# A gated linear attention with an MLP behind it: q and k of the later blocks transposed by DMA instead of by TensorE

## The chip, the cores and the metric

The kernel runs on one core of a Trainium2 chip. A core has four engines that compute (TensorE, or PE, for matmuls; VectorE, or DVE; ScalarE, or ACT; GpSimd, or POOL), a fifth, SyncE (SP), that only issues transfers and waits, and 16 DMA engines that all queues share. Every engine runs its own instructions in order. The metric is the device time of one execution in microseconds (us), lower is better.

## What is computed

For 4 batches and 8 heads of size 48, over 768 steps, a state of 48 by 48 is decayed row by row and updated, and read with q. The outputs of the 8 heads, side by side (384 numbers per token, 3,072 tokens), go through an MLP with a squared ReLU:

```python
for t in range(S):
    state = alpha[:, :, t, :, None] * state + np.einsum('bhd,bhe->bhde', k[:, :, t], v[:, :, t])
    y[:, :, t] = np.einsum('bhd,bhde->bhe', q[:, :, t], state)
...
h = x @ w_in                     # 384 -> 2048
r = np.maximum(h, 0.0)
g = s * (r * r) + b
return (g @ w_out).astype(np.float32)   # 2048 -> 384
```

Inputs and output are float32; the kernel computes its matmuls in bfloat16.

## The kernel before

The 768 steps of a batch are cut into 6 chunks of 128 steps, which makes 24 blocks n of 128 tokens (n // 6 is the batch, n % 6 the chunk). Within a block the recurrence is done in parallel form, and between the blocks of one batch a state is carried on. Names in capitals: NBLK is 24, NCH is 6, NP is 4 (pairs of heads), NLD is 8 (depth of the rings of loads).

For one block the steps are functions, each with one or a few engines:

- `load(n)`: four DMAs from SyncE, alpha, k, q and v, of 192 KB each, in pieces of 192 bytes (one head of one token).
- `ln` (ScalarE), `cum` (one matmul with a triangle of ones, and two exponentials on ScalarE into `bi_sb` and `b_sb`): the running product of the decays and its inverse. For blocks from the sixth on, `cum` ends with `decay(n)`: the last row of `b_sb` is stored to a row in DRAM and fetched back, spread over partitions, as `blast`; three small DMAs from SyncE, the second and third of which wait for the first to land. The last chunk of a batch needs none.
- `vcast` (GpSimd): v to bfloat16.
- `qk` (VectorE): k times `bi_sb` into `kb_sb` and q times `b_sb` into `qb_sb`, each 128 tokens by 8 heads of 64 columns (48 used).
- `tr`: eight transposes on TensorE (L244), four pairs of heads for q and four for k, into the PSUM tile `ct_ps`, and one copy on VectorE (L249) into `qkT_sb`.
- `amat`: eight matmuls from `qkT_sb` (L259) and two multiplications by a mask on VectorE (L267).
- `y` (`yp` and `st`): what the block reads from the carried state (L278) and from itself (L287), the block's contribution to the state (L298), the eviction of y on ScalarE (L305, `y_bf`), and the update of the state on VectorE (L334) and GpSimd (L339, L343), which reads `blast`.
- `xt`: three transposes of `y_bf` and an eviction on ScalarE into `xd_all`.
- `m(n, u)`, u from 0 to 3: the first product of the MLP (`mp`, L365, 12 matmuls), ReLU on ScalarE (`rl`, L379) and the square on VectorE (`sq`, L386).
- `o(n, u)`: the second product (`mm2`, L402, 4 matmuls). After u = 3 a block below the fourteenth is copied by ScalarE into `keep_sb`, which lies over the float32 staging of the first weights; it gets its bias later by `add_bias` (VectorE, L441) and is stored then. Later blocks get their bias from PSUM at once (VectorE, L415) and are stored. All stores were issued by SyncE (L438); the last block's two halves too (L435).

The order is written out by hand: the first blocks as a list, and from the fifth on by positions, `p = 8 * n` for the y of block n, and every other step at an offset from it. The steps are sorted by position and issued; each engine gets its part of that order, and a framework puts the semaphores between engines. For n of 8 and up the offsets are: `ln` p - 16.7, `cum` p - 14.8, `qk` p - 14.6, `tr` p - 10.8, `amat` p - 7.9, `load(n + 5)` p - 4, `y` p, `xt` p + 1, `m` p + 2.5, 3.5, 5.5 and 7.5, `o` p + 8.5, 9.5, 12.5 and 14.5. So one block's attention overlaps the MLP of the two blocks ahead of it. `add_bias` and the stores of the first 13 blocks stand at fixed positions from 117.3 and 118.2 on, 5.5 apart.

Of the kernel before, what the change touches and what calls it, by code (L numbers as in the profile page):

```python
# [9 lines left out]
BF16 = mybir.dt.bfloat16  # L10
# [4 lines left out]
def kernel(  # L15
# [25 lines left out]
    UNITS = 5  # L41
    assert sum(GROUPS) == NBLK
    NLD = 8

    ctx.enter_context(tc.manual_schedule())
    sb = ctx.enter_context(tc.tile_pool(name="sb", bufs=1))
# [32 lines left out]
    la_sb = ring("la_sb", [128, H, 64], BF16, 2)  # L79
    b_sb = ring("b_sb", [128, H, 48], FP32, 2)  # L80
    bi_sb = ring("bi_sb", [128, H, 48], FP32, 2)
    qb_sb = ring("qb_sb", [128, H, 64], BF16, 2)
    kb_sb = ring("kb_sb", [128, H, 64], BF16, 3)
    v_bf = ring("v_bf", [128, H, 48], BF16, 3)
    y_bf = ring("y_bf", [128, H * 48], BF16, 2)
    qkT_sb = ring("qkT", [128, 2, NP, 128], BF16, 2)
    am_sb = [ring("am_a", [128, NP, 128], BF16, 2), ring("am_b", [128, NP, 128], BF16, 2)]
    blast = ring("blast", [128, NP, 1], FP32, 3)
    row_dr = [dr.tile([1, H * 48], FP32, name=f"row_dr{i}") for i in range(3)]
# [118 lines left out]
    def cum(n):  # L208
        la = la_sb[n % 2]
        nc.tensor.matmul(out=cum_ps, lhsT=U_bf, rhs=la[:, :, 0:48], start=True, stop=True)  # L210
# [12 lines left out]
        if n < NCH - 1:  # L223
            nc.scalar.activation(out=blast[n % 3][0:112, :, 0], in_=tot_ps[0:112], func=AF.Exp)
        elif n % NCH < NCH - 1:
            decay(n)

    def decay(n):
        row = row_dr[n % 3]
        nc.sync.dma_start(out=row, in_=b_sb[n % 2].rearrange("s h d -> s (h d)")[127:128])  # L230
        for e in range(2):
            nc.sync.dma_start(
                out=blast[n % 3][64 * e : 64 * e + 48, :, 0],
                in_=row.rearrange("o (p e d) -> e d (o p)", e=2, d=48)[e],
            )

    def qk(n):
        nc.vector.tensor_tensor(out=kb_sb[n % 3][:, :, 0:48], in0=k_sb[n % NLD], in1=bi_sb[n % 2], op=ALU.mult)  # L238
        nc.vector.tensor_tensor(out=qb_sb[n % 2][:, :, 0:48], in0=q_sb[n % NLD], in1=b_sb[n % 2], op=ALU.mult)  # L239

    def tr(n):
        for x, t in ((0, qb_sb[n % 2]), (1, kb_sb[n % 3])):
            for p in range(NP):
                nc.tensor.transpose(  # L244
                    out=t_ps[0:112, x, p, :],
                    in_=t.rearrange("a h d -> a (h d)")[:, 128 * p : 128 * p + 112],
                    identity=ident,
                )
        nc.vector.tensor_copy(  # L249
            out=qkT_sb[n % 2][0:112].rearrange("a x p t -> a (x p t)"),  # L250
            in_=t_ps[0:112].rearrange("a x p t -> a (x p t)"),
        )

    def amat(n):
        qkT = qkT_sb[n % 2]
        for p in range(NP):
            for e in range(2):
                r0 = 64 * e
                nc.tensor.matmul(  # L259
                    out=a_ps[e][:, p, :],  # L260
                    lhsT=qkT[r0 : r0 + 48, 1, p, :],
                    rhs=qkT[r0 : r0 + 48, 0, p, :],
                    start=True,
                    stop=True,
                )
        for e in range(2):
            nc.vector.tensor_tensor(out=am_sb[e][n % 2], in0=a_ps[e], in1=mask4, op=ALU.mult)  # L267
# [6 lines left out]
    def yp(n):  # L274
        c = n % NCH
        if c > 0:
            for p in range(NP):
                nc.tensor.matmul(  # L278
                    out=y_ps[:, 96 * p : 96 * p + 96],
                    lhsT=qkT_sb[n % 2][0:112, 0, p, :],  # L280
                    rhs=sd_sb[(n - 1) % 2][0:112, p, :],
                    start=(p == 0),
                    stop=False,
                    skip_group_check=True,
                )
        for h in range(H):
            nc.tensor.matmul(  # L287
                out=y_ps[:, 48 * h : 48 * h + 48],
                lhsT=am_sb[h % 2][n % 2][:, h // 2, :],
                rhs=v_bf[n % 3][:, h, :],  # L290
                start=(c == 0 and h == 0),
                stop=(h == H - 1),
                skip_group_check=True,
            )
        if c < NCH - 1:
            kb = kb_sb[n % 3].rearrange("a h d -> a (h d)")
            for p in range(NP):
                nc.tensor.matmul(  # L298
                    out=pst[:, p, :],
                    lhsT=kb[:, 128 * p : 128 * p + 128],  # L300
                    rhs=v_bf[n % 3][:, 2 * p : 2 * p + 2, :],
                    start=True,
                    stop=True,
                )
        nc.scalar.activation(out=y_bf[n % 2], in_=y_ps[:, 0 : H * 48], func=AF.Copy)  # L305
# [88 lines left out]
    def mm2(g, t, u):  # L394
# [14 lines left out]
        if u == 3:  # L409
            if g < NKEEP:  # L410
                nc.scalar.activation(out=keep_sb[g], in_=op[:, 0:d_model], func=AF.Copy)
                return
            ot = out_sb[nout[0] % 3]
            nout[0] += 1
            nc.vector.tensor_tensor(out=ot, in0=op[:, 0:d_model], in1=bias_w, op=ALU.add)  # L415
            store(g, ot)


    def last(u):
# [14 lines left out]
                nc.vector.tensor_tensor(out=ot[:, 0:hc], in0=op[half][:, 0:hc], in1=bias_w[:, cols], op=ALU.add)  # L434
                nc.sync.dma_start(out=out[(NBLK - 1) * C : NBLK * C, cols], in_=ot[:, 0:hc])  # L435

    def store(n, o):
        nc.sync.dma_start(out=out[n * C : (n + 1) * C, :], in_=o)  # L438

    def add_bias(n):  # L440
        nc.vector.tensor_tensor(out=keep_sb[n], in0=keep_sb[n], in1=bias_w, op=ALU.add)  # L441
# [21 lines left out]
    for t in la_sb:  # L463
        nc.vector.memset(t, 0.0)
    nc.vector.memset(ones_c, 1.0)
    for t in qb_sb + kb_sb + blast:
        nc.vector.memset(t, 0.0)
    make_identity(nc, ident)
    for i in range(NP):
# [8 lines left out]
    def at(pos, fn, *args):  # L478
        events.append((pos, len(events), fn, args))
# [54 lines left out]
        at(111.5 + 2 * i, bias_row, i)  # L534
    for n in range(NKEEP):
        at(117.3 + 5.5 * n, add_bias, n)
        at(118.2 + 5.5 * n, store, n, keep_sb[n])
    for u in range(1, 4):
        at((30.5, 31.2, 32.5)[u - 1], o, 3, u)
    at(20.0, load, NLD)  # L540
    for n in range(4, NBLK):
        p = 8 * n
        if n > 4:
            f = min((n - 5) / 3.0, 1.0)
            c, t, a = 9.0 + 5.8 * f, 5.8 + 5.0 * f, 3.4 + 4.5 * f
# [12 lines left out]
        at(p + 1.0, xt, n)  # L558
    for _, _, fn, args in sorted(events, key=lambda e: e[:2]):
        fn(*args)  # L560
# [30 lines left out]
```

## Time and profile before

| what | value |
|---|---|
| time, median of 3 runs | 199.65 us (199.53 to 199.88) |
| profiled execution: span from first to last instruction | 198.2 us |
| what the median lies above that span | 1.45 us |
| TensorE busy | 185.2 us, 93% |
| VectorE busy | 150.8 us, 76% |
| ScalarE busy | 118.8 us, 60% |
| GpSimd busy | 64.2 us, 32% |
| bytes moved by DMA | 30.33 MB, 153 GB/s in the mean |
| transposes of q and k on TensorE (L244) | 192 matmuls, 19.9 us busy, pipelined |
| copies of them on VectorE (L249) | 24, 685 ns each |

The profiled execution's own time is known by its span only. A page of the profile gives the busy time by engine, the span in 40 slices, the DMA queues, the chain that ended last, and the costliest groups of instructions. In the lines, PE is TensorE's matmul, PEld its weight load, DVE, ACT, POOL and SP the other engines; a q behind the name (SPq, ACTq) is the engine's sequencer, which issues transfers and waits. "x8" is the number of instructions in a line; "L244" is a line of the kernel. A line of the chain or the timeline begins with its start in us from the span's start and its length in us.

### The profile page before, as it was taken

The numbers are of one execution on the slowest core, as the hardware profiler recorded it, in microseconds if no ns is written. First come the engines' busy times: TensorE is split into PE (matmuls) and PEld (weight loads), VectorE is DVE, ScalarE is ACT, GpSimd is POOL, SyncE is SP. The second block draws the span as 40 slices with busy tenths as digits, with TensorE's granted clock in tenths as the row PEclk, the third lists the DMA queues.
The fourth block names the chain that finished last, engine by engine and source line by source line (L and its number), as shares of the span: only waits on it lengthen the run. The fifth ranks groups of instructions, "written<-read, shape, count | busy, mean of one in ns | idle before, by whom it ended". The sixth has DMA issues, their size and how long they took to land.

```text
span 198.2 us, 6120 instructions
## 1 busy us (share of the span) xinstructions
PE 185.2 (93%) x2440; PEld 145.3 (73%) x2440; DVE 150.8 (76%) x296; ACT 118.8 (60%) x243; POOL 64.2 (32%) x96
## 2 busy tenths in 40 slices
PE   1999899988899999999999999999999999999994
PEld 1566587754577688888878877878888877877783
DVE  5467777867466779789877996989987999998532
ACT  3245668381675765766766677666575665664650
POOL 5142251611120136326500633623700851652000
PEclk9999999999999999999999999999999999999999
DMA  7999999999999384693968846958947953122212
GB/s 125 189 342 232 314 283 369 199 177 193 187 172 195 60 142 86 101 159 64 195 84 148 134 68 120 159 93 193 229 87 164 161 176 112 41 82 81 87 37 79
DMA packets 113454, 30.33 MB, mean 153 GB/s; under 512 B 106627, under 2 KB 111890, under 8 KB 113426
## 3 DMA queue, kind: packets, MB, share of 16 engines
q1 hardware_dynamic: 109262, 29.15, 73.7%
q10 hardware_dynamic: 4164, 0.79, 2.8%
q8 instruction: 19, 0.31, 0.7%
q14 instruction: 9, 0.07, 0.1%
HBM read 25.19 MB, written 4.74 MB: 151 GB/s over the span
## 4 chain that ended last, share of the span: by engine, by line
PE 68%; SPq 15%; DMA 10%; DVE 3%; ACT 1%; issue 1%; ACTq 0%; DVEq 0%
PE h_ps L365 25%; PE o_ps L402 25%; DMA q_sb<-in_q_dram 8%; SPq L128 5%; PE ct_ps L244 5%; SPq L147 4%; PE a_ps L259 3%; SPq L125 3%; SPq L122 2%; PE ct_ps L210 2%; PE y_ps L287 2%; PE h_ps L312 2%; DMA al_sb<-in_alpha_dram 2%; SPq L131 1%; PE a_ps L425 1%; PE y_ps L278 1%
## 5 line engine op out<-in xcount | busy, mean ns | idle before, releaser
L379 ACT ACTIVATE r_sb<-h_ps 128x512 bf16<-128x512 f32 x94 | 55.8, 597 | 39.2 <-PE h_ps L365 37.6
L365 PE MATMUL h_ps<-xd_all,w_in_bf 128*128 128x128 bf16 x1128 | 74.8, 219 | 1.5 <-ACT r_sb L379 1.1
L365 PEld LDWEIGHTS <-w_in_bf 128*128 128x128 bf16 x1152 | 69.3, 98 | 8.4 <-issue 2.3
L402 PE MATMUL o_ps<-w_out_bf,gt_all 128*128 128x384 bf16 x336 | 68.5, 326 | 1.4 <-DVE w_out_bf L160 0.7
L386 DVE TENSOR_TENSOR gt_all<-r_sb 128x512 bf16<-128x512 bf16 x96 | 45.3, 484 | 26.5 <-ACT r_sb L379 25.8
L339 POOL TENSOR_TENSOR sd_sb<-t_sb,blast 48x192 bf16<-48x192 f32 x40 | 22.5, 563 | 103.5 <-DVE t_sb L334 67.3
L402 PEld LDWEIGHTS <-gt_all 128*128 128x128 bf16 x368 | 32.5, 98 | 17.4 <-issue 1.8
L343 POOL TENSOR_TENSOR sc_sb<-t_sb,blast 112x384 f32<-112x384 f32 x16 | 21.8, 1362 | 1.3
L206 POOL CAST v_bf<-v_sb 128x384 bf16<-128x384 f32 x24 | 17.7, 744 | 12.9 <-DMA v_sb<-in_v_dram 12.7
L318 ACT ACTIVATE xd_all<-h_ps 128x384 bf16<-128x384 bf16 x24 | 11.8, 490 | 15.5 <-PE h_ps L312 15.5
L249 DVE COPY qkT<-ct_ps 112x1024 bf16<-112x1024 bf16 x24 | 16.4, 685 | 4.8 <-PE ct_ps L244 4.7
L238 DVE TENSOR_TENSOR kb_sb<-k_sb,bi_sb 128x384 bf16<-128x384 f32 x24 | 13.7, 569 | 8.3 <-ACT bi_sb L221 8.2
L267 DVE TENSOR_TENSOR am_a<-a_ps,mask 128x512 bf16<-128x512 f32 x24 | 16.4, 683 | 3.1 <-PE a_ps L259 3.1
L239 DVE TENSOR_TENSOR qb_sb<-q_sb,b_sb 128x384 bf16<-128x384 f32 x24 | 16.7, 694 | 0.0
L267 DVE TENSOR_TENSOR am_b<-a_ps,mask 128x512 bf16<-128x512 f32 x24 | 16.3, 681 | 0.0
L221 ACT ACTIVATE bi_sb<-ct_ps 128x384 f32<-128x384 f32 x24 | 11.7, 487 | 5.2 <-PE ct_ps L213 3.9
L305 ACT ACTIVATE y_bf<-y_ps 128x384 bf16<-128x384 f32 x24 | 11.7, 488 | 4.9 <-PE y_ps L287 4.8
L203 ACT ACTIVATE la_sb<-al_sb 128x384 bf16<-128x384 f32 x24 | 12.4, 516 | 3.6 <-DMA al_sb<-in_alpha_dram 3.6
L210 PE MATMUL ct_ps<-la_sb,U_bf 128*128 128x384 bf16 x24 | 8.2, 340 | 4.6 <-ACT la_sb L203 4.6
L222 ACT ACTIVATE b_sb<-ct_ps 128x384 f32<-128x384 f32 x24 | 11.9, 494 | 0.0
L244 PEld LDWEIGHTS <-qb_sb 128*112 128x112 bf16 x96 | 8.5, 136 | 4.4 <-DVE qb_sb L239 3.2
L259 PE MATMUL a_ps<-qkT 48*128 48x128 bf16 x192 | 10.2, 226 | 1.0 <-DVE qkT L249 0.4
(66 smaller groups left out, 195.0 us busy)
## 6 DMA issues: line engine op xcount, KB each, us to landing
al_sb<-in_alpha_dram SPq DMA_DIRECT2D x24, 192.0 KB, 3.2
k_sb<-in_k_dram SPq DMA_DIRECT2D x24, 192.0 KB, 3.6
q_sb<-in_q_dram SPq DMA_DIRECT2D x22, 192.0 KB, 4.7
v_sb<-in_v_dram SPq DMA_DIRECT2D x22, 192.0 KB, 4.9
w_in_st<-in_moe_w_in_dram SPq DMA_DIRECT2D x4, 768.0 KB
w_out_st<-in_moe_w_out_dram SPq DMA_DIRECT2D x4, 768.0 KB
out_dram<-w_in_st SPq DMA_DIRECT2D x13, 192.0 KB, 2.6
out_dram<-out_sb SPq DMA_DIRECT2D x10, 192.0 KB, 3.4
```

What stands on the lines that cost most here:

```text
L206: nc.gpsimd.tensor_copy(out=v_bf[n % 3], in_=v_sb[n % NLD])
L239: nc.vector.tensor_tensor(out=qb_sb[n % 2][:, :, 0:48], in0=q_sb[n % NLD], in1=b_sb[n % 2], op=ALU.mult)
L244: nc.tensor.transpose(out=t_ps[0:112, x, p, :], in_=t.rearrange("a h d -> a (h d)")[:, 128 * p : 128 * p + 112], identity=ident,)
L249: nc.vector.tensor_copy(out=qkT_sb[n % 2][0:112].rearrange("a x p t -> a (x p t)"), in_=t_ps[0:112].rearrange("a x p t -> a (x p t)"),)
L259: nc.tensor.matmul(out=a_ps[e][:, p, :], lhsT=qkT[r0 : r0 + 48, 1, p, :], rhs=qkT[r0 : r0 + 48, 0, p, :], start=True, stop=True,)
L267: nc.vector.tensor_tensor(out=am_sb[e][n % 2], in0=a_ps[e], in1=mask4, op=ALU.mult)
L339: nc.gpsimd.tensor_tensor(out=sd[r, :, d], in0=t1_sb[r, :, d], in1=bl[r].to_broadcast([48, NP, 48]), op=ALU.mult)
L343: nc.gpsimd.tensor_tensor(out=sc_sb[0:112], in0=t1_sb[0:112], in1=bl[0:112].to_broadcast([112, NP, 96]), op=ALU.mult)
L365: nc.tensor.matmul(out=hp[:, jj * N : (jj + 1) * N], lhsT=w_in_bf[:, kk, 128 * j : 128 * (j + 1)], rhs=xd_sb[g][:, kk, 0:N], start=(kk == ...
L379: nc.scalar.activation(out=rs, in_=h_of.pop((g, u)), func=AF.Relu)
L386: nc.vector.tensor_tensor(out=gt_sb[g][:, u * 512 : (u + 1) * 512], in0=rs, in1=rs, op=ALU.mult)
L402: nc.tensor.matmul(out=op[:, 0:d_model], lhsT=gt_sb[g][:, j * N + t * C : j * N + (t + 1) * C], rhs=w_out_bf[:, j, :], start=(j == 0), sto ...
```

## The change

The blocks below the ninth stay as they were. From block 8 on (`TDMA = 8`) the eight transposes on TensorE and the copy on VectorE are replaced by one DMA transpose of the whole tile of scaled q and k, 128 partitions by 1,024 bfloat16, which SyncE issues at p - 14.55, right behind `qk`. For that, `qb_sb` and `kb_sb` become the two halves of one tile `qk_sb`, in a ring of three, and `qkT_sb` gets a third buffer. `amat` of these blocks moves from p - 7.9 to p - 6.0.

The decay is cut in two: the store of the row stays in `cum`, and the two fetches become a step of their own, `decay(n)`, at p - 10.0 for n of 8 and up, behind the load at p - 12; for blocks 5 to 7 it stands just behind `qk`, where no other instruction of SyncE lies between.

Every store but the last block's is issued by ScalarE instead of SyncE, at a position of its own: for the kept blocks 2.0 behind `add_bias` (0.9 before), for the later ones at p + 16.2, behind the last `o` at p + 14.5.

```diff
+    TDMA = 8
...
-    qb_sb = ring("qb_sb", [128, H, 64], BF16, 2)
-    kb_sb = ring("kb_sb", [128, H, 64], BF16, 3)
+    qk_sb = ring("qk_sb", [128, 2, H, 64], BF16, 3)
+    qb_sb = [t[:, 0] for t in qk_sb]
+    kb_sb = [t[:, 1] for t in qk_sb]
...
-    qkT_sb = ring("qkT", [128, 2, NP, 128], BF16, 2)
+    qkT_sb = ring("qkT", [128, 2, NP, 128], BF16, 3)
...
         elif n % NCH < NCH - 1:
-            decay(n)
+            nc.sync.dma_start(out=row_dr[n % 3], in_=b_sb[n % 2].rearrange("s h d -> s (h d)")[127:128])

     def decay(n):
         row = row_dr[n % 3]
-        nc.sync.dma_start(out=row, in_=b_sb[n % 2].rearrange("s h d -> s (h d)")[127:128])
+        if n < NCH - 1 or n % NCH == NCH - 1:
+            return
         for e in range(2):
             nc.sync.dma_start(
...
+    def tr_dma(n):
+        nc.sync.dma_start_transpose(
+            out=qkT_sb[n % 3].rearrange("a x p t -> a (x p) t"),
+            in_=qk_sb[n % 3].rearrange("a x h d -> a (x h d)"),
+        )
...
             nc.vector.tensor_tensor(out=ot, in0=op[:, 0:d_model], in1=bias_w, op=ALU.add)
-            store(g, ot)
+            finished[g] = ot
...
-    def store(n, o):
-        nc.sync.dma_start(out=out[n * C : (n + 1) * C, :], in_=o)
+    finished = {n: keep_sb[n] for n in range(NKEEP)}
+
+    def store(n):
+        nc.scalar.dma_start(out=out[n * C : (n + 1) * C, :], in_=finished.pop(n))
...
-    for t in qb_sb + kb_sb + blast:
+    for t in qk_sb + blast:
         nc.vector.memset(t, 0.0)
...
-        at(118.2 + 5.5 * n, store, n, keep_sb[n])
+        at(119.3 + 5.5 * n, store, n)
...
-            at(p - t, tr, n)
-            at(p - a, amat, n)
+            if n < TDMA:
+                at(p - t, tr, n)
+                at(p - a, amat, n)
+            else:
+                at(p - c + 0.25, tr_dma, n)
+                at(p - 6.0, amat, n)
+            at(p - 10.0 if n >= TDMA else p - c + 0.3, decay, n)
...
+        if NKEEP <= n < NBLK - 1:
+            at(p + 16.2, store, n)
```

Here c is 14.8 for n of 8 and up.

More of the change, by code (lines that the diff above doesn't have):

```diff
@@ L238, in qk @@
         nc.vector.tensor_tensor(out=kb_sb[n % 3][:, :, 0:48], in0=k_sb[n % NLD], in1=bi_sb[n % 2], op=ALU.mult)
-        nc.vector.tensor_tensor(out=qb_sb[n % 2][:, :, 0:48], in0=q_sb[n % NLD], in1=b_sb[n % 2], op=ALU.mult)
+        nc.vector.tensor_tensor(out=qb_sb[n % 3][:, :, 0:48], in0=q_sb[n % NLD], in1=b_sb[n % 2], op=ALU.mult)
+    def tr_dma(n):
[3 more added lines that the diff above has]
+        )
     def tr(n):
-        for x, t in ((0, qb_sb[n % 2]), (1, kb_sb[n % 3])):
+        for x, t in ((0, qb_sb[n % 3]), (1, kb_sb[n % 3])):
             for p in range(NP):
@@ L249, in tr @@
         nc.vector.tensor_copy(
-            out=qkT_sb[n % 2][0:112].rearrange("a x p t -> a (x p t)"),
+            out=qkT_sb[n % 3][0:112].rearrange("a x p t -> a (x p t)"),
             in_=t_ps[0:112].rearrange("a x p t -> a (x p t)"),
@@ L254, in amat @@
     def amat(n):
-        qkT = qkT_sb[n % 2]
+        qkT = qkT_sb[n % 3]
         for p in range(NP):
@@ L279, in yp @@
                     out=y_ps[:, 96 * p : 96 * p + 96],
-                    lhsT=qkT_sb[n % 2][0:112, 0, p, :],
+                    lhsT=qkT_sb[n % 3][0:112, 0, p, :],
                     rhs=sd_sb[(n - 1) % 2][0:112, p, :],
```

## The prediction

> **What bounds the kernel now.** I read the page first, then the chain that ended last within one steady block, then the engines' timeline of that block, and last SyncE's queue and the busy time by stretch. The page says which engine is full:
>
> ```profile
> PE 185.2 (93%) x2440; PEld 145.3 (73%) x2440; DVE 150.8 (76%) x296; ACT 118.8 (60%) x243; POOL 64.2 (32%) x96
> PEclk9999999999999999999999999999999999999999
> DMA  7999999999999384693968846958947953122212
> ```
>
> PE is TensorE. It is full after the first third, and its granted clock is at the top all along. The busy time by stretch, where the figure after PEclk's 1.00 is the DMA engines' mean busy share and the last one GB/s:
>
> ```profile
> 45.00:50.00 5.00, 3.80 (x32) 1.98 (x30) 3.52 (x6) 1.44 (x4) 0.51 (x1) 1.00 1.31 192
> 70.00:77.00 7.00, 7.00 (x103) 5.75 (x101) 5.75 (x13) 4.77 (x11) 2.86 (x5) 1.00 0.68 118
> 77.00:84.00 7.00, 7.00 (x104) 5.75 (x101) 5.49 (x11) 4.71 (x11) 3.19 (x5) 1.00 0.72 115
> ```
>
> From 70 us on PE is busy 7.00 us of 7.00; VectorE (5.5 to 5.8) and ScalarE (4.7 to 4.8) have room. Around 45 us the loads fill the DMA engines instead, at 192 GB/s; from 70 us the same loads need 115 to 118 GB/s. The chain within one block, restricted to 87 to 95 us:
>
> ```profile
> 87.75 0.20 PE y_ps L287 x8
> 87.95 0.17 PE p_ps L298 x4
> 88.13 0.33 PE a_ps L259 x8
> 88.46 0.76 PE o_ps L402 x4
> 89.21 0.17 PE h_ps L312 x3
> 89.38 0.16 PE ct_ps L210
> 89.54 0.65 PE o_ps L402 x4
> 90.19 1.34 PE h_ps L365 x24
> 91.53 0.65 PE o_ps L402 x4
> 92.18 0.45 PE ct_ps L244 x8
> ```
>
> Nothing but PE work, end to end: one block takes 7.04 us (two calls of y start 87.42 and 94.45), and 0.45 us of it is the eight transposes at L244. Whatever leaves PE leaves the block, as long as its replacement arrives in time. So the question is when a transposed tile lands, and that goes through SyncE's queue. Six lines of its timeline (start, length, issue):
>
> ```profile
> 83.58 0.44 SPq L122 DMA_DIRECT2D al_sb<-in_alpha_dram  x1
> 84.11 0.53 SPq L128 DMA_DIRECT2D k_sb<-in_k_dram  x1
> 84.73 0.81 SPq L125 DMA_DIRECT2D q_sb<-in_q_dram  x1
> 85.60 0.72 SPq L131 DMA_DIRECT2D v_sb<-in_v_dram  x1
> 86.42 0.58 SPq L230 DMA_DIRECT2D row_dr<-b_sb  x1
> 89.59 1.81 SPq L232 DMA_DIRECT2D blast<-row_dr  x2
> ```
>
> A load of 192 KB holds the queue for 0.4 to 0.8 us, and after the row store SyncE waits for its landing (86.42 + 0.58 to 89.59): the waits by SyncE list 30.2 us for that, in 15 waits.
>
> **The change, part by part.** Block 8 is the first changed one; its y starts near 80.4 us (87.42 less 7.04), its transposes stand in the chain at 71.07 us. Nothing before about 70 us changes but the fills (three of 2 KB a partition for five of 1 KB, at 0.27 us each for 1 KB: 0.3 us more, near 3 us, where VectorE has nothing else until bi_sb at 5.2): the decay of blocks 5 to 7 is issued at the same place among SyncE's instructions.
>
> *Off PE.* Of the 16 sets of transposes, 15 stand in the chain: eleven at 0.45, three at 0.50, one at 0.51, together 6.96 us. The sixteenth (near 121 us, where the chain runs through VectorE) counts 0.45. Gain 7.4 us.
>
> *Off VectorE.* Sixteen copies at L249, 0.685 us each, 11 us. VectorE is not the bound, so most of it is worth nothing. At 118.8 to 121.9 us the chain passes r_sb, gt_all, qkT (0.60) and cs_sb before PE goes on with L184, where PE and its weight load waited 0.2 and 0.6 us. With the copy gone I count 0.3 us of gain.
>
> *The transposed tile by DMA: its time on the DMA engines, X.* The tile is 128 partitions of 2 KB, 256 KB, and no row shows such a transfer. Lower end: its bytes at the highest rate of any slice, 369 GB/s, give 0.71 us. Near row: at 45 to 50 us, with queues full, a 192 KB load takes 196.6 KB / 192 GB/s = 1.02 us (187 GB/s at 50 to 55 us: 1.05); scaled by bytes 1.06 x 256/192 = 1.4 us. Upper end: twice a load, 2.1 us, since both ends of the transfer lie in SBUF. A far row would be one piece per element: 131,072 elements at the loads' 1,024 pieces in 1.06 us are 136 us a tile; I leave that out of the range because the instruction is a transposing form and not a strided copy. I take 1.4, from the loads, the nearest row in pieces and bytes.
> [...]
>
> *Does it land in time?* tr_dma(10) can be issued when qb of block 10 is done: L239 started at 83.80 and takes 0.55, so 84.35. amat(10) now stands after y(9), two output products, xt and cum, just ahead of the first mp of block 9. That mp starts at 90.03; less 0.33 for amat, which used to stand ahead, and 0.45 for the transposes in between: 89.25. The window is 4.9 us. A DMA of 0.8 KB (blast) lands 1.9 us after issue, so the transposed tile needs 1.9 + 1.4 = 3.3 us when nothing is queued ahead, with 1.6 us to spare. Then the masks at L267 (2 x 0.68) still have over 2 us before y(10) at 94.0, but qk of block 11 now goes ahead of them on VectorE; both fit.
>
> *What is queued ahead.* On SyncE the transfer stands between row store and loads, so ahead of it in the queue is the load set issued right after the transfer of the block before. New block period: 7.04 - 0.45 = 6.59 us. DMA time in one: four loads 4.25 us, small ones 0.1, X 1.4, sum 5.75: it drains. From the first store (L438 at 133.23 us) also 2.45 stores a block; at 350 GB/s, as the weights moved in the early slices, 0.56 us each, 1.4 us. (4.25 + 0.1 + 1.4 = 5.75 of 7.04 is a share of 0.82, which is what 130 to 140 us shows.) With X: 7.15, or 0.56 over the period. Only three load sets follow the first store (136.65, 145.19, 153.03 us), so the lag grows to 1.7 us against 1.6 to spare: 0.1 us of PE wait. After that there are no loads.
>
> *SyncE's own time.* Four loads about 2.7 us with gaps, two decay fetches 0.8, row store 0.3: 3.8 us, and the hold h of the transpose. A load's issue holds 0.44 to 0.99 us where the queue isn't full; twice the longest, 2.0, is the upper end. At h = 1.2, between, the sum is 5.0 of 6.59 and SyncE waits for qk again, as it now waits for the row. Behind that wait stand only the next loads, five blocks early, and the decay fetch.
>
> *Decay behind the loads.* It loses its 2 us wait on the row. It lands behind a load set, about 1 + 1.4 + 4.25 us after the transfer's issue near 84.4, so by about 92; POOL's sd_sb of that block runs 1.9 us after y, near 96. Four us of cover; without it POOL and then the next y would wait. Cost 0.
>
> *Stores from ScalarE.* 23 issues of 0.33 to 0.40 us. ACTq shows what an issue does: at 18.33 a load's issue (0.38) ran beside the activation that started at 18.35 (0.49), so one issue hides under the activation ahead of it. ScalarE also idles about 2 us a block (1.17, 0.29 and 0.70 us in the one shown). The wait for VectorE's add is two positions after it, and the add is behind no late work there: at most 0.3 us where it meets the masks that moved. I count 0.2 in all; bounds 0 and 23 x 0.35 = 8, the latter only if PE waited for each.
>
> *xt closer to y.* amat used to stand between y and the output product that covers y_bf. y_bf of block 9 ends 1.29 us after y's start (88.71), and PE now reaches xt after 1.30. In block 23, which already runs so, the weight load waited 0.35 us for y_bf and PE lost 0.13. I count 0.1 for the five blocks 8 to 12, whose ScalarE also evicts outputs: 0.5.
>
> Sum: -7.4 - 0.3 + 0.1 + 0.2 + 0.5 = -6.9 us. The profiled execution has a span of 198.2, so the new span is 191.3; the median of the runs, 199.65, lies 1.45 us above that span, which I keep: **192.8 us**.
>
> **Rivals.** *Late tiles or small stalls eat part.* X at 2.1: before the stores 6.45 a block still fits; with them 7.85, so 3 x 1.26 = 3.8 less 0.9 to spare: 195.5. With h near 2.5, or ScalarE's issues a third exposed (2.7 us), 195 to 199. For it: the window has 1.6 us to spare only. Against: 30 us of SyncE waits vanish.
>
> *Slower: the transpose costs the DMA engines (or SyncE) over 2.6 us.* Nine load sets follow the first transfer ahead of the stores, three behind. Extra time: 9 (4.35 + X - 6.59) + 3 (5.75 + X - 6.59) - (4.9 - 1.9 - X); that is 7 us at X = 2.5 to 2.6, from where it decides. At X = 3.2 it is 15.7 us: 208 us. For it: neighbouring two-byte elements of the output come from different partitions, and loads in 192-byte pieces already move at half the rate of the weights (192 against 369 GB/s). Against: X would be three loads' time. The same holds if h is over 6.59 - 3.8 = 2.8 us.
> [...]
>
> *No change.* The 0.45 us come back as a wait of xt for y_bf plus exposed issues, 16 times. For it: block 23's 0.35 us. Against: it lost 0.13 only.
>
> **How the numbers follow.** Hidden as forecast, 191.5 (X = 0.7, no stalls, 0.5 of them avoided) to 195.5 (X = 2.1): 0.62. Partly eaten, 195.5 to 199.2: 0.14. No change: 0.03. Slower: 0.21, of which about half lies below 204. The range leaves out about 0.05 at the low end's side and 0.12 at the upper: 191.2 to 203. The likeliest case's own range is 191.5 to 195.5. Faster 0.76, same 0.03, slower 0.21, where 0.2% (0.4 us) is about what can be told from no change.
>
> **What would show it.** Right: no L244 after 70 us, blocks 6.6 us apart, PE still full, the transposed tile landing within 4.9 us, SyncE waiting for qb_sb instead of row_dr. Wrong: PE's weight load at L259 waiting for a DMA into qkT, period set by DMA share near 1.0 or by one long SPq issue; PEld L312 waiting 0.4 us for y_bf in each block; r_sb late behind ACTq issues. The prediction falls if X or h exceeds 2.6 us.

## The result and the profile after

The changed kernel takes 202.06 us in the median, against 199.59 us for the kernel before on the same chip: a ratio of 1.0105, with a 95% interval of 1.0075 to 1.0134. It is slower by 1%, where 3.4% faster was forecast. The profiled execution has a span of 199.7 us, 1.5 us more than the 198.2 before. The profiled executions already differ ahead of everything that was edited: y of block 5 starts at 57.7 to 61.1 us, and in e1, e7, e10, e12 and e15 TensorE's granted clock is 0.67 to 0.73 from 20 to 25 us, so the traces are compared here from y(5), the y of block 5, on.

Busy time by engine, the granted clock and the DMA engines' share, on the page of the changed kernel:

```profile
PE 180.7 (90%) x2312; PEld 135.4 (68%) x2312; DVE 142.2 (71%) x278; ACT 119.0 (60%) x243; POOL 58.7 (29%) x96
PEclk9999999999999999999999999999999999999999
DMA  6999999999999299979998998697999855425112
```

The 128 transposes are gone from TensorE (2,440 instructions before, 2,312 now), and VectorE has lost 8.6 us of work. Yet the span did not shrink: TensorE is no longer full. The clock is not the reason. One stretch that was shown of before, and two long ones (columns: length, busy time of PE, PEld, DVE, ACT and POOL with counts, granted clock, DMA share, GB/s):

```profile
70.00:77.00 7.00, 5.30 (x66) 3.69 (x63) 4.77 (x10) 4.50 (x10) 3.27 (x6) 1.00 0.98 161
...
90.00:140.00 50.00, 47.71 (x641) 36.05 (x640) 39.12 (x72) 33.94 (x72) 16.50 (x24) 1.00 0.94 163
140.00:183.00 43.00, 41.34 (x553) 31.57 (x553) 35.48 (x71) 26.54 (x55) 14.41 (x20) 1.00 0.72 163
```

From 90 to 183 us TensorE now idles 3.9 us; before it idled 0.3 us there. Two different losses stand behind this.

**The first tile is late.** SyncE's timeline as block 8 comes up:

```profile
69.42 0.44 SPq L124 DMA_DIRECT2D al_sb<-in_alpha_dram  x1
...
71.14 0.90 SPq L133 DMA_DIRECT2D v_sb<-in_v_dram  x1
72.54 0.47 SPq L228 DMA_DIRECT2D row_dr<-b_sb  x1
73.13 2.12 SPq L245 DMA_TRANSPOSE qkT<-qk_sb  x1
```

VectorE finished qb of block 8 at 70.02 us, but SyncE was still working off row, decay and a load set, and reached the transfer only at 73.13. The chain of work goes through it (start, length):

```profile
73.13 4.62 DMA qkT<-qk_sb
...
77.80 0.40 PE a_ps L268 x8
```

TensorE waited 2.5 us for this tile. From y of block 7 to y of block 8 it is 9.33 us (72.79 to 82.12), against 7.04 before. No later tile is waited for. How much this costs hangs on how far TensorE is ahead of SyncE's queue: in the run e15 below, which is the same up to here, SyncE issues this transfer at nearly the same time (73.63), but TensorE is 3 us later (y(7) at 75.80 instead of 72.79) and does not wait.

**The blocks do not get shorter.** From y(8) to y(23) it is 105.66 us (82.12 to 187.78); before it was 106.02 (80.38 to 186.40). So fifteen blocks together gained 0.4 us, where the 14 sets of transposes that stood among them (those of blocks 10 to 23), at 0.45 us each, should have given 6.3. The early ones take 6.76 us, later ones 6.7 to 7.9. The early ones, to y(11), are still TensorE's work from end to end, as before. Against the forecast 7.04 - 0.45 = 6.59 they are 0.17 us longer, and the chain of block 9 shows where:

```profile
89.59 0.65 PE o_ps L411 x4
90.24 0.34 PE h_ps L321 x3
90.58 0.16 PE ct_ps L212
```

The three matmuls of `xt` took 0.17 us before (89.21, L312); now that `amat` no longer stands between y and `xt`, their weights, `y_bf`, come late. The chain inside one of the long ones:

```profile
133.44 0.49 ACT bi_sb L223
...
134.67 1.18 DVE qk_sb L242
135.84 0.60 DVE am_a L276
136.44 0.60 DVE am_b L276
...
137.37 0.47 DVE w_in_st L452
...
139.43 0.48 DVE out_sb L424
...
139.95 0.81 PE o_ps L411 x4
```

In the block shown of before, this list held nothing but TensorE. Here it runs from the exponential `bi_sb` through VectorE's q times `b_sb`, the masks, the squares (between the lines shown) and the biases of two outputs, and only then to the product on TensorE. VectorE, busy for 71% of the span, sets the end of this block because of the order of its work. That order is easiest to see in a block without the biases. One block of VectorE before the change (y of block 9 starts at 87.42):

```profile
88.71 0.55 DVE L334 TENSOR_TENSOR t_sb<-p_ps,sc_sb 112x384 f32<-112x384 f32 x1
89.17 0.68 DVE L267 TENSOR_TENSOR am_a<-a_ps,mask 128x512 bf16<-128x512 f32 x1
89.77 0.68 DVE L267 TENSOR_TENSOR am_b<-a_ps,mask 128x512 bf16<-128x512 f32 x1
90.37 0.55 DVE L238 TENSOR_TENSOR kb_sb<-k_sb,bi_sb 128x384 bf16<-128x384 f32 x1
90.84 0.55 DVE L239 TENSOR_TENSOR qb_sb<-q_sb,b_sb 128x384 bf16<-128x384 f32 x1
91.59 1.41 DVE L386 TENSOR_TENSOR gt_all<-r_sb 128x512 bf16<-128x512 bf16 x2 [0.20 <-ACT r_sb L379]
```

And the same block after it (y of block 9 starts at 88.88; in brackets the idle time ahead and who ended it):

```profile
90.17 0.55 DVE L343 TENSOR_TENSOR t_sb<-p_ps,sc_sb 112x384 f32<-112x384 f32 x1
91.52 0.78 DVE L241 TENSOR_TENSOR qk_sb<-k_sb,bi_sb 128x384 bf16<-128x384 f32 x1 [0.79 <-ACT bi_sb L223]
92.22 1.18 DVE L242 TENSOR_TENSOR qk_sb<-q_sb,b_sb 128x384 bf16<-128x384 f32 x1
93.32 0.68 DVE L276 TENSOR_TENSOR am_a<-a_ps,mask 128x512 bf16<-128x512 f32 x1
93.92 0.68 DVE L276 TENSOR_TENSOR am_b<-a_ps,mask 128x512 bf16<-128x512 f32 x1
94.52 0.75 DVE L395 TENSOR_TENSOR gt_all<-r_sb 128x512 bf16<-128x512 bf16 x2
```

`t_sb` comes 1.29 us after y in both. Before, the two masks stood next and filled the time in which ScalarE made `bi_sb`. Now `qk` stands ahead of the masks, VectorE idles 0.79 us for `bi_sb`, the multiplication by q takes 1.18 instead of 0.55 us, and the squares behind it start 5.64 us after y instead of 4.17. In this block TensorE did not wait for VectorE; it does where VectorE has the sums of the bias or the outputs to add as well. Summed over the run, in the list of waits (us in total, times, longest):

```profile
DVE qk_sb L241 <- ACT bi_sb L223: 19.8, 20, 2.2
PEld L321 <- ACT y_bf L314: 6.2, 15, 0.7
PE o_ps L411 <- DVE out_sb L424: 2.6, 5, 1.2
PE a_ps L268 <- DMA qkT<-qk_sb: 2.5, 1, 2.5
```

Before, VectorE waited 8.2 us in 7 waits for `bi_sb`, the weight load of `xt` 1.6 us in 4 for `y_bf`, and TensorE never for `out_sb`. Most of those waits of before lie in the first 70 us, which did not change; from 70 us on it is 12.6 us in 15 waits for `bi_sb` instead of 0.6 in 2, and 5.2 us in 13 for `y_bf` instead of 0.6 in 2.

### The profile page after: what moved, and what is told of

The parts are those of the page before. It is cut to its first block, busy times and chain, and to the rows that moved or that the text cites. A ratio compares the mean times of both kernels' runs of the same rounds, so it can differ in the third digit from the quotient of the medians.

```text
span 199.7 us, 5851 instructions
## 1 busy us (share of the span) xinstructions
PE 180.7 (90%) x2312; PEld 135.4 (68%) x2312; DVE 142.2 (71%) x278; ACT 119.0 (60%) x243; POOL 58.7 (29%) x96
## 4 chain that ended last, share of the span: by engine, by line
PE 52%; DVE 15%; ACT 6%; issue 5%; DMA 2%; ACTq 0%; DVEq 0%
PE o_ps L411 20%; PE h_ps L374 19%; DVE qk_sb L242 3%; DVE gt_all L395 3%; PE h_ps L321 3%; PE a_ps L268 2%; DMA qkT<-qk_sb 2%; ACT r_sb L388 2%; DVE am_b L276 2%; DVE am_a L276 2%; ACT bi_sb L223 1%; DVE out_sb L424 1%; PE y_ps L296 1%; PE a_ps L434 1%; DVE w_out_bf L162 1%
## 5 line engine op out<-in xcount | busy, mean ns | idle before, releaser
L374 PEld LDWEIGHTS <-w_in_bf 128*128 128x128 bf16 x1152 | 68.6, 98 | 10.0 <-issue 2.1
L348 POOL TENSOR_TENSOR sd_sb<-t_sb,blast 48x192 bf16<-48x192 f32 x40 | 23.7, 592 | 110.4 <-DVE t_sb L343 69.1
L395 DVE TENSOR_TENSOR gt_all<-r_sb 128x512 bf16<-128x512 bf16 x96 | 39.0, 422 | 23.3 <-ACT r_sb L388 22.8
L411 PEld LDWEIGHTS <-gt_all 128*128 128x128 bf16 x368 | 33.1, 98 | 18.9 <-issue 4.9
L241 DVE TENSOR_TENSOR qk_sb<-k_sb,bi_sb 128x384 bf16<-128x384 f32 x24 | 16.1, 671 | 19.8 <-ACT bi_sb L223 19.8
L242 DVE TENSOR_TENSOR qk_sb<-q_sb,b_sb 128x384 bf16<-128x384 f32 x24 | 21.0, 875 | 0.1
L208 POOL CAST v_bf<-v_sb 128x384 bf16<-128x384 f32 x24 | 16.9, 713 | 13.1 <-DMA v_sb<-in_v_dram 12.9
L352 POOL TENSOR_TENSOR sc_sb<-t_sb,blast 112x384 f32<-112x384 f32 x16 | 15.9, 994 | 1.3
L268 PEld LDWEIGHTS <-qkT 48*128 48x128 bf16 x192 | 5.7, 97 | 11.6 <-issue 5.9
L195 PE MATMUL o_ps<-mask,U_bf 128*128 128x512 bf16 x28 | 10.3, 468 | 0.0
```

What stands on the lines that cost most here:

```text
L208: nc.gpsimd.tensor_copy(out=v_bf[n % 3], in_=v_sb[n % NLD])
L242: nc.vector.tensor_tensor(out=qb_sb[n % 3][:, :, 0:48], in0=q_sb[n % NLD], in1=b_sb[n % 2], op=ALU.mult)
L268: nc.tensor.matmul(out=a_ps[e][:, p, :], lhsT=qkT[r0 : r0 + 48, 1, p, :], rhs=qkT[r0 : r0 + 48, 0, p, :], start=True, stop=True,)
L348: nc.gpsimd.tensor_tensor(out=sd[r, :, d], in0=t1_sb[r, :, d], in1=bl[r].to_broadcast([48, NP, 48]), op=ALU.mult)
L352: nc.gpsimd.tensor_tensor(out=sc_sb[0:112], in0=t1_sb[0:112], in1=bl[0:112].to_broadcast([112, NP, 96]), op=ALU.mult)
L374: nc.tensor.matmul(out=hp[:, jj * N : (jj + 1) * N], lhsT=w_in_bf[:, kk, 128 * j : 128 * (j + 1)], rhs=xd_sb[g][:, kk, 0:N], start=(kk == ...
```

## The experiments

My theory after the result was that the transfer works as priced and that the loss is the move of `amat` from p - 7.9 to p - 6.0 (an order of VectorE's work), plus one late tile. Rivals: the transfers crowd the DMA engines or SyncE; the stores on ScalarE; the tile not in time in many blocks. All ratios are to the kernel before, with 95% intervals.

**The late tile: loads behind it.** Against the changed kernel:

```diff
-            at(p - 4.0, load, n + NLD - 3)
+            at(p + 1.5 if n >= 6 else p - 4.0, load, n + NLD - 3)
```

> The changed kernel (202.06 us) with each load set from the twelfth block on moved from p - 4 to p + 1.5, just behind the transposing transfer of two blocks on. Queue theory (SyncE is late and a load set stands ahead of the first transfer, so PE waits 2.5 to 2.9 us once, near 73 us): that wait goes, 199.2 to 199.8 us, and the first transfer lands about 3 us after its issue instead of 4.6. Order theory (amat's new place is what costs) and transfer theory (the transfers slow the DMA engines and all loads): 201.5 to 202.1 us, since neither hangs on where the loads are issued.

Measured: 202.7 us, 1.012 (1.0079 to 1.0162). The stall at block 8 was gone, 6.76 us from y(7) to y(8) instead of 9.33, and the kernel was no faster: one tile was late once later (1.6 us of TensorE), and over the run `y_bf` was still waited for 16 times (6.8 us) and `bi_sb` 20 times (21.8 us). TensorE was also 1.7 us later in this trace (y(7) at 74.47), which alone would make the stall smaller; that the edit does its part is seen in e4 below, where TensorE is as early as in the changed kernel (y(7) at 72.82) and SyncE issues the transfer at 70.39 instead of 73.13. Removing the most visible wait did not touch the larger loss.

**The order alone, in the kernel before.** `amat` at p - 6.0 with all transposes still on TensorE:

```diff
-            at(p - a, amat, n)
+            at(p - (6.0 if n >= 8 else a), amat, n)
```

> The kernel before (199.6 us; TensorE transposes, no transposing transfers) with only amat of the ninth and later blocks at p - 6.0. Order theory: the same waits of xt for y_bf and of VectorE for bi_sb appear, 0.2 to 0.45 us a block over 16 blocks: 202.5 to 206 us. Transfer theory: no change, 199.4 to 199.9 us.

Measured: 205.19 us, 1.0262 (1.0238 to 1.0286). The waits of this run:

```profile
DVE kb_sb L238 <- ACT bi_sb L221: 18.0, 18, 2.4
PEld L312 <- ACT y_bf L305: 5.7, 14, 0.7
PE o_ps L402 <- DVE out_sb L415: 1.8, 5, 0.5
```

These are the waits of the changed kernel, in a kernel with no transfer, no new queue and stores where they were. The move alone costs 2.6%, 5.2 us, and the trace puts it behind y(5): from there to y(23) it takes 133.5 us instead of 128.4. This is the central experiment.

**A place in between, in the kernel before:**

```diff
-            at(p - a, amat, n)
+            at(p - (6.65 if n >= 8 else a), amat, n)
```

> The kernel before with amat of the ninth and later blocks at p - 6.65: behind xt and cum on PE, but with its masks still ahead of qk on VectorE. At p - 6.0 it had cost 5.1 us (205.2). If that was the wait of xt for y_bf: 203.5 to 205.5 us again. If it was VectorE's order (waiting for bi_sb with the masks behind): 200 to 202 us, and kb_sb waits for bi_sb less than 3 us in all instead of 12.7.

Measured: 208.12 us, 1.0393 (1.0362 to 1.0423), which neither theory had. Here the masks stand ahead of `qk`, so from 70 us on the wait for `bi_sb` is gone, but `qb_sb` is late for TensorE's transposes (7.0 us of weight loads in 12 waits) and `y_bf` is still waited for (5.6 us in 15). Later is not better by degrees: each place puts another pair of steps in the wrong order.

**The changed kernel with `amat` earlier.**

```diff
-                at(p - 6.0, amat, n)
+                at(p - 7.3, amat, n)
```

> The changed kernel with amat at p - 7.3 instead of p - 6.0: on PE it then stands between the first output product and xt, on VectorE its masks go ahead of qk, as before the change. Order theory: xt no longer waits for y_bf (6.2 us in 15 waits), VectorE no longer waits 19.8 us for bi_sb, blocks take 6.6 to 6.8 us instead of 7.05, so 4 to 6 us less over 15 blocks, less about 1 us for the first transfer, which is needed earlier: 197 to 199 us. Transfer theory: the tiles are needed 1.2 us earlier and come too late in each block: 203 us or more, with PE's weight load at amat waiting for the transfer.

Measured: 208.39 us, 1.0427 (1.038 to 1.0473), which is what the rival with the late tiles had forecast for this run. The wait of `xt` is gone (0.4 us left from 70 us on), but the tile is late:

```profile
PEld L268 <- DMA qkT<-qk_sb: 14.5, 9, 5.6
```

So with `qk` at p - 14.6, the position 7.3 is too early for the transfer and 6.0 too late for VectorE. Where the tile was in time, blocks took 6.59 to 6.60 us (87.53, 94.13, 100.72): the forecast block exists.

**Both edits, e1 and e2 together**, two changed lines:

```diff
+                at(p - 7.3, amat, n)
...
+            at(p + 1.5 if n >= 6 else p - 4.0, load, n + NLD - 3)
```

> Both edits, loads behind the transfer and amat at p - 7.3. Queue and order theory together: 2.3 us and 4 to 6 us less, the sum of the two: 194 to 196.5 us, blocks of 6.6 to 6.7 us. Order theory alone: 197 to 199. Transfer theory: 202 us or more.

Measured: 204.36 us, 1.0219 (1.0164 to 1.0273). Blocks of 6.59 to 6.60 us where the tile is in time, and 11.5 us of waits of the weight load for it, 12 times (longest 2.7). This too is the rival's figure: with `qk` where it was, the time from `qk` to `amat` is too short for the transfer.

**No transfer in the changed kernel:**

```diff
-    TDMA = 8
+    TDMA = 24
```

What stays of the change is the stores on ScalarE and the shared rings; `amat` is back at p - 7.9.

> The changed kernel with every block transposed by TensorE again and amat and decay at the places of before; what stays of the change is the stores on ScalarE and the shared tile in a ring of three. Order and transfer theories: as before, 199.4 to 200.2 us. If the stores on ScalarE cost: 200.5 to 203 us.

Measured: 200.43 us, 1.0052 (1.0011 to 1.0094). The trace does not put this half per cent down to the stores or the rings: from y(5) to y(23) it takes 128.5 us (60.54 to 189.06), as before (128.4), and what it loses lies ahead of y(5). The changed kernel takes 129.9 us there (57.90 to 187.78), so its loss belongs to the pair of transfer and move.

**Stores back on SyncE in the changed kernel:**

```diff
-        nc.scalar.dma_start(out=out[n * C : (n + 1) * C, :], in_=finished.pop(n))
+        nc.sync.dma_start(out=out[n * C : (n + 1) * C, :], in_=finished.pop(n))
```

> The changed kernel with its stores issued by SyncE again, at the same positions. If the stores on ScalarE cost nothing and relieve SyncE: 202 to 206 us, as SyncE waits for VectorE's add ahead of the next transfer. If ScalarE's issues and waits are part of what is lost: 199.5 to 201.5 us.

Measured: 204.21 us, 1.0224 (1.0161 to 1.0287), worse than the change. The trace does not put this down to the stores: TensorE waited 5.1 us for `qkT` in 3 waits, but 3.2 of it at block 8 (11.57 us from y(7) to y(8)), more than 50 us ahead of the first of the stores that moved (136.4). From y(8) to y(23), with the stores, it takes 105.6 us against 105.7: 1.9 us of late tiles, and 1.1 us of waits for `out_sb` instead of 2.6. So these runs do not show that moving the stores off SyncE helped this kernel.

**No loads after the thirteenth block.** The load steps of blocks 13 to 23 are left out, so these blocks compute with the data of eight blocks earlier; everything else runs.

```diff
-        if n + 5 < NBLK:
+        if n + 5 < 13:
```

> The changed kernel with the loads of blocks 13 to 23 left out (they compute with the data of eight blocks earlier, so part of the work of the DMA engines is missing and nothing else). Transfer theory (loads, stores and transfers crowd the DMA engines or SyncE's queue): blocks from about 85 us on take 6.6 us, 194 to 196 us. Order theory: the waits of xt, of VectorE for bi_sb and of PE for the output buffer stay, 199.5 to 202 us.

Measured: 204.03 us, 1.0162 (1.0095 to 1.023). A stretch, and the waits after 84 us (columns as above):

```profile
100.00:140.00 40.00, 38.09 (x513) 28.91 (x511) 31.01 (x58) 27.09 (x57) 11.84 (x17) 1.00 0.29 57
```

```profile
DVE qk_sb L241 <- ACT bi_sb L223: 11.8, 14, 1.6
PEld L321 <- ACT y_bf L314: 4.3, 11, 0.6
PE o_ps L411 <- DVE out_sb L424: 2.5, 5, 1.1
```

The DMA engines' share was 0.29 from 100 to 140 us, where with all loads it is 0.94 (90 to 140), and y(9) to y(23) took 98.7 us (89.31 to 188.00) against 98.9 with all loads. The blocks of the changed kernel do not hang on the DMA engines' load. (The run as a whole is no faster because its first stretch was slower: y(5) came at 60.9 instead of 57.9 us, ahead of anything that the edit touches.)

**Giving the transfer its time: `qk` and decay earlier.** If the tile needs more lead and `amat` must stay at p - 7.9, then `ln`, `cum`, `qk` and transfer must move ahead. e5 does so by a ramp:

```diff
+            if n >= TDMA:
+                c = min(14.8 + 1.6 * (n - 7), 22.8)
...
-                at(p - 6.0, amat, n)
-            at(p - 10.0 if n >= TDMA else p - c + 0.3, decay, n)
+                at(p - 7.9, amat, n)
+            at(p - c + 4.8 if n >= TDMA else p - c + 0.3, decay, n)
```

> The changed kernel with ln, vcast, cum, qk, the transfer and the decay of the ninth and later blocks moved ahead step by step (1.6 positions more for each block) until they stand one block earlier, at p - 22.8 instead of p - 14.8, and with amat back at p - 7.9, where it was before the change. Order and window theory (the transfer as such is cheap; its price was that amat had to move to give it time): the window grows to more than 10 us, no weight load waits for the transfer, blocks take 6.6 us and the time is 193.5 to 196 us. Transfer theory: the DMA engines stay the bound, 200 us or more.

Measured: 203.59 us, 1.0161 (1.0075 to 1.0247). Blocks of 6.5 to 6.6 us almost everywhere, so the order is right now; what remains is the first tile (3.5 us of TensorE) and two holes of 2.5 and 2.8 us in ScalarE, ahead of `y_bf` and `xd_all`, each put down to a DMA, each with a store next to it.

The same with stores on SyncE (e9), with transfers from block 10 only (e10), with both (e11), and as a control both with all transposes on TensorE (e12, `TDMA = 24`):

> The kernel with qk one block earlier and amat back at p - 7.9 (fastest 201.9 us), with the stores issued by SyncE instead of ScalarE. In that kernel's trace ScalarE stood still for 2.5 and 2.8 us near 148 and 157 us until a decay fetch had landed, just ahead of a store; in the program each store is preceded by a wait for an older transfer that used the same one of eight completion counters. If that is the cause: those two waits go, 198 to 199.5 us, and the wait at the first transfer (4.2 us) stays. If not: 201.5 to 204 us, or more as SyncE is held by the adds.

> The same kernel (stores on ScalarE), with the ninth and tenth blocks transposed by TensorE again, so that the first transfer falls to a block that already has the long window. Queue theory: the one wait of 4.2 us near 80 us goes, for 0.9 us more of TensorE work: 198 to 199.5 us. If the wait only moves to the eleventh block: 201.5 to 204 us.

> Both of these: stores on SyncE, first transfer at the eleventh block. If the three causes (window, first transfer, stores on ScalarE) are all there is: blocks of 6.6 us from the eleventh on, 193.5 to 196 us, which beats the kernel before (199.6). If the transfers themselves cost more on the DMA engines than is hidden: 198 us or more, with blocks over 6.8 us while loads run.

> A control: qk one block earlier and stores on SyncE at the new positions, but every block transposed by TensorE as before the change, no transposing transfer. If the gain of the run with both edits comes from TensorE's transposes leaving: 199.3 to 200.5 us, as before. If it comes from the earlier qk: 194 to 197 us here as well.

Measured: e9 202.11 us, 1.0059 (1.0023 to 1.0095); e10 203.76 us, 1.0183 (1.012 to 1.0247); e11 202.47 us, 1.0117 (1.0053 to 1.0181); e12 202.27 us, 1.0099 (1.0067 to 1.0132). In e9 ScalarE's two holes are gone, but TensorE waits 6.1 us for three tiles, 3.8 of it for the first. In e10 no tile is late, but ScalarE is held again (`y_bf` 4.0 us in 4 waits from 70 us on). In e11 ScalarE is free, but the stores stand ahead of transfers on SyncE and TensorE waits 4.3 us for `qkT` in 3 waits. e12 shows a price of the preparation: its steady blocks are as before (y(8) to y(23) 105.93 us), but y(5) to y(8) takes 24.58 instead of 22.38 us. One queue at a time was relieved at the other's cost.

**Stores behind the last load.** e11 with the bias and the stores of the first 13 blocks later and closer together:

```diff
-        at(117.3 + 5.5 * n, add_bias, n)
-        at(119.3 + 5.5 * n, store, n)
+        at(140.3 + 3.8 * n, add_bias, n)
+        at(142.3 + 3.8 * n, store, n)
```

> The kernel with qk one block earlier, the first transfer at the eleventh block and stores on SyncE (201.4 us at the fastest), with the bias adds and stores of the first 13 blocks moved behind the last load (from 140.3 and 142.3 on, 3.8 apart, instead of 117.3 and 119.3, 5.5 apart). There three tiles were late, 4.5 us in all, two of them while loads and stores shared SyncE's queue. If the late tiles come from that sharing: they land in time, 196.5 to 198.5 us. If they come from the transfers themselves: 200.5 to 203 us.

Measured: 200.56 us, 1.0016 (0.9977 to 1.0056). One late tile is left: TensorE waits 1.8 us for it, the granted clock is 0.79 in the five us behind (95 to 100), and that block takes 10.06 us. e4 with late stores on SyncE (e14) tests whether that is enough without the ramp:

> The run with both edits (loads behind the transfer, amat at p - 7.3; 203.5 us at the fastest), with the stores on SyncE and those of the first 13 blocks behind the last load. Sharing of the queue: part of its 11.5 us of late tiles goes, 198 to 201 us. Window theory: the tiles are late by 1 us a block even with the loads alone, 202 to 204 us.

Measured: 203.87 us, 1.0154 (1.0088 to 1.022). It is not.

**The version that beats both.** e13 with the transfers from block 12 and a ramp that starts where SyncE has caught up:

```diff
-    TDMA = 10
+    TDMA = 12
...
-            if n >= 8:
-                c = min(14.8 + 1.6 * (n - 7), 22.8)
+            if n >= 10:
+                c = min(14.8 + 2.0 * (n - 9), 22.8)
```

> As the run with stores behind the last load, but with two more blocks transposed by TensorE and the step to one block earlier made from the eleventh block on (2.0 positions a block): 0.9 us more of TensorE work, against the 2.2 us that the control lost up to the ninth block by moving work ahead there. If that loss comes from where the work is moved ahead, 196 to 198 us; if it comes whenever it is moved, 198 to 200 us.

Measured: 196.83 us (196.55 to 197.29), 0.9839 (0.9806 to 0.9873). Span 195.5 us. Its stretches:

```profile
90.00:140.00 50.00, 49.91 (x683) 39.63 (x680) 39.69 (x74) 35.70 (x76) 17.68 (x26) 1.00 0.98 161
140.00:183.00 43.00, 43.00 (x600) 34.76 (x597) 35.69 (x73) 26.71 (x53) 15.93 (x20) 1.00 0.74 162
```

TensorE is full again, at a DMA share of 0.98; no engine waits for a DMA into `qkT`, and the blocks from 131 us on are 6.5 to 6.6 us apart (those from 116 to 131, with the bias sums among them, 7.1 to 7.3). It still pays for the preparation: from y(5) to y(11) it takes 44.95 us instead of 43.50. Two controls on it. With all transposes on TensorE:

```diff
-    TDMA = 12
+    TDMA = 24
```

> This is the kernel with transfers from block 13 and the decay, qk and masks moved ahead by the ramp, stores late on SyncE (196.8 us), with one edit: no transfer, all transposes on TensorE. If the gain of that kernel comes from the transposes leaving TensorE (11 or 12 blocks, 0.49 us of TensorE's work and what is queued behind it in each), this one is slower than it by 2.7 to 5 us: 199.5 to 201.5. If it comes from the earlier decay and qk or from the late stores alone, it stays at about 197.

Measured: 202.43 us, 1.0095 (1.005 to 1.014). With the same order and the same stores the twelve transfers are worth the difference of the two ratios, 1.0095 - 0.9839, or 5.1 us of 200, 0.43 us a block. The two traces say the same: y(11) to y(23) takes 79.5 us (103.53 to 183.06) with transfers and 84.5 (104.23 to 188.72) without. And e16 with its stores on ScalarE:

```diff
-        nc.sync.dma_start(out=out[n * C : (n + 1) * C, :], in_=finished.pop(n))
+        nc.scalar.dma_start(out=out[n * C : (n + 1) * C, :], in_=finished.pop(n))
```

> The same kernel (196.8 us) with its stores issued by ScalarE instead of SyncE, at the same places. If a store on ScalarE is held until landings of older transfers, as the idle stretches of 2.5 and 2.8 us of ScalarE in the run with the earlier qk let suppose, some blocks are longer by one to three us and the time is 197.2 to 199.5, with ScalarE's idle time put down to a DMA. If ScalarE's issues are only their own issue time, it is 196.5 to 197.2.

Measured: 203.89 us, 1.0136 (1.0032 to 1.0239). Of the 49 us from 90 to 139 TensorE idles 1.1, of the 19 from 139 to 158 it idles 2.6, at a clock of 1.00; with the stores on SyncE it was 0.1 in 93. From SyncE's timeline, and from ScalarE's (in brackets the idle time ahead and what ended it):

```profile
155.74 0.61 SPq L130 DMA_DIRECT2D k_sb<-in_k_dram  x1
```

```profile
156.70 0.50 ACT L224 ACTIVATE b_sb<-ct_ps 128x384 f32<-128x384 f32 x1
160.27 0.34 ACTq L449 DMA_DIRECT2D out_dram<-w_in_st  x1
160.99 1.09 ACT L388 ACTIVATE r_sb<-h_ps 128x512 bf16<-128x512 f32 x2 [3.79 <-DMA k_sb<-in_k_dram]
```

ScalarE stands still for 3.8 us ahead of a store of an output that has nothing to do with k. What ends its wait is the landing of a load that SyncE issued at 155.74 and that took 4.45 us, and the ReLU behind the store waits with it. (Behind this hole the granted clock falls to 0.66 for 5 us, so part of this kernel's time comes from there.) The built program of e18 gives a reason, which I have read there and not measured apart: its 188 transfers, of both queues, use eight completion counters in turn, and this store, the eighth transfer behind that load, first waits for the counter that the two share. So here a store on ScalarE waited for a load of SyncE.

## Why the prediction was wrong

**Failed: the place of `amat`.** The step that decided was half a sentence under "Does it land in time?": "qk of block 11 now goes ahead of them on VectorE; both fit". They fit as a sum of busy time, not as an order: with `qk` ahead, VectorE waits for `bi_sb` with the masks and the squares behind it. I priced the move at nothing there and at 0.5 us under "xt closer to y" (0.1 us in five blocks). Measured alone it costs 5.2 us (e3), with `y_bf` late 12 times from 70 us on, by 0.4 us in the mean, instead of in the five blocks that I counted. My text named "PEld L312 waiting 0.4 us for y_bf in each block" as a sign of failure; it came, 5.2 us in 13 waits from 70 us on.

**Failed, smaller: "Does it land in time?"** I took SyncE as free when `qb` is done. For some later blocks it nearly is (at 135.91 us the transfer is issued 0.06 us after `qb`). For block 8 it was 3.1 us behind (70.02 to 73.13), because the decay and loads of earlier blocks had kept it; the trace of before already showed SyncE late there, and I had looked at 83 to 91 us only. The margin of 1.6 us was gone and 2.5 us of TensorE's time with it. How large this loss is was in part luck: 3.2 us of waiting in e6 and none in e15, with the same instructions up to there.

**Right: "Off PE" and "Off VectorE" as work.** 7.4 us for 16 blocks is 0.46 a block; the twelve transfers of e16 are worth 0.41 to 0.43 a block against e17. The forecast block of 6.59 us appears in e2, e4, e13 and e16.

**Right: X, h and the landing.** The transfer lands 3.1 us after issue in the median (3.3 forecast) and holds SyncE 1.24 us (1.2 taken), 2.12 for the first, with the DMA engines' share at 0.96 to 1.06 from 70 to 80 us. X alone was not measured; the time of the DMA engines' packets grew by 21 us for 16 transfers from before to the changed kernel, and by 25 us for 12 from e17 to e16, which makes X an estimated 1.3 to 2.1 us (1.4 taken, 2.1 my upper end). The upper rival's condition of 2.6 us was not met, and the slower rival, whose sign was right, had the wrong cause: e15 shows the blocks unchanged at less than a third of the DMA share. (Its sum at X = 3.2 is 15.9 us, not 15.7.) In the same trace the 192 KB loads of alpha, q and v land after 3.0 to 4.7 us, those of k after 8.3 (medians).

**Right: decay behind the loads.** SyncE's wait for the row fell from 30.2 to 3.4 us, and no block waited long for `blast` after the first.

**Half right: stores from ScalarE at 0.2 us.** From y(5) to y(23) e7, with these stores and the old order, takes 128.5 us against 128.4 before. But in e18 the stores on ScalarE cost 3.0% against e16 (1.0136 to 0.9839): not by their 0.35 us of issue, which I had counted, but by a wait for landings of the other queue, which I had not.

**The sum.** Forecast -6.9 us, measured +1.5 in the span: a miss of 8.4. From y(7) to y(8), where one set of transposes less should have given -0.5, it was +2.3: 2.8 of the miss. From y(8) to y(23) the 14 sets and the small terms made -6.0, and it was -0.4: 5.6. What TensorE itself met there accounts for about 5.4 us: it idled 3.2 us for results of VectorE (`out_sb` and `cs_sb`) and 0.7 for `y_bf`, and the matmuls of `xt`, at up to 0.35 us instead of 0.17, took some 1.5 us more (an estimate, summed from the chain's lines). Read so, the larger part went to "both fit", a term that I had put at nothing, and some 2.2 us to "xt closer to y", which I had put at 0.5. Of my rivals "No change" had the second mechanism (the 0.45 us come back at `xt`); I gave it 0.03, because the one block that showed the wait lost only 0.13 us. That size was about right, 0.17; it came in many more blocks than I counted. No rival had VectorE's order.

## What to carry to other kernels

Here 0.45 us a block left the full engine and fifteen blocks together gained 0.4 us, as the order on another engine had changed. So when a step moves, write out for each in-order engine what now stands ahead of what, and what that one waits for, instead of adding up busy time. Before a new transfer is put on a queue, look at where that queue stands at the first use (here 3.1 us behind), not in a steady block. And test a move by itself in the old kernel (e3, where it cost 5.2 us): it tells in one run whether the loss comes from the new thing or from making room for it.

## What the runs showed of the hardware

- VectorE's multiplications of two SBUF tiles and GpSimd's `sc_sb` took longer beside each other. In the changed kernel the one by `b_sb`, 0.55 us in the block of before, started at 92.22, while GpSimd's `sc_sb` ran from 91.96 to 92.98, and took 1.18 us; so it did in all ten blocks from 70 us on in which `sc_sb` had started first, and it took 0.55 us in the two where GpSimd did nothing beside it (105.62 and 149.37). Before, VectorE came first (kb and qb from 90.37 to 91.39) and `sc_sb`, from 90.50, took 1.58 us instead of 1.02. So in these blocks the order of work between the two engines also decided who paid, and in the long block shown VectorE paid on the critical path (1.18 us at 134.67).
- Behind four of the six waits of TensorE for a tile that are listed here the granted clock was lower, and such a wait cost more than itself. In e2 (a wait of 5.2 us) TensorE did 0.62 us of work from 75 to 80 us, and the granted clock was 0.86 there and 0.50 in the next five; in e9 (3.8 us; 1.40 us of work) and e6 (3.2 us; 1.75) it was 0.85 and 0.83, then 0.81 and 0.83; in e13 (1.8 us; 3.23 us of work from 90 to 95 us) it was 0.86, then 0.79. After the wait of 2.5 us of the changed kernel and that of 3.5 of e5 no slice shows less than full clock. The length of the wait alone does not order them, so these runs give no threshold.
- Open: why the preparation costs 2.2 us from y(5) to y(8) in e12 and 1.45 from y(5) to y(11) in e16. And no run parts the loss at `y_bf` from the loss by VectorE's order; the split above is read from what TensorE waited for in one trace.
